# Which engine issues the loads of q, k, v and the stores, in a fused attention and expert kernel

## The chip, the cores and the metric

The kernel runs on one core of a Trainium2 chip. The core has a matrix engine (TensorE; PE in the profile, PEld its weight loads), VectorE (DVE), ScalarE (ACT), GpSimd (POOL) and SyncE (SP), each with its own instruction queue, which it works off in order, and 16 DMA engines, which move data between the device's memory (DRAM) and the on-chip memory (SBUF). An engine that issues a DMA does so at that place of its queue: if the DMA has to wait, say for a buffer to be free, all that stands behind it in the queue waits too. The metric is the time of one execution on the device in microseconds (us), lower is better.

## The reference

Three parts, all in float32, one after the other:

```
A  = softmax(q  @ mean18(k)^T / 8)          q, k, v: 4 batches x 8 heads x 576 tokens x 64
Bm = softmax(mean18(q) @ mean18(k)^T / 8)   mean18: means of 18 tokens, so 32 landmarks
C  = softmax(mean18(q) @ k^T / 8)
Z  = six Newton steps  Z <- 2Z - Z Bm Z     (pseudo-inverse of Bm)
x  = A Z C v                                2304 tokens x 512
e  = argmax of normalised x against 8 expert embeddings;  g = its softmax weight
x  = g * relu(x @ w1[e]) @ w2[e]            w1: 512 x 1024
x  = rmsnorm(x) * rms_g
out = (silu(x @ w_gate) * (x @ w_val)) @ w_out      512 -> 1536 -> 512
```

## The kernel before, in words

Batches b = 0 to 3 go through the first two parts one behind the other, and the stages of several batches overlap. A batch is handled in two halves of four heads (`hh`).

- `load` (L247) brings k and q of one half, 128 rows of 18 x 64 numbers (4,608 contiguous bytes a row, 576 KB), into one of two buffers each. `loadv` (L254) brings v of a batch, 1.1 MB, into the one v buffer: 128 rows with 8 runs of 1 KB each, and a tail of 64 rows with 8 runs of 256 bytes.
- `turn` (L262) transposes k and q on VectorE, `sums` (L277) makes the landmark sums (for batches 0 and 1 on TensorE, L285, later on VectorE or GpSimd, L310 to L315), `crow` (L334) computes C and its product with v (`pv`, L398), `inverse` (L406) the Newton steps (L465), `arow` (L542) the rows A. L598 in `arow` normalises these on GpSimd; TensorE then transposes them (L610).
- `pair` (L726) splits the turned rows into two float16 parts, `etp`, and stores them to DRAM as `ed`, and the small matrix WTb as `wd`. These copies are read again only by a slow path at the end (L1077, L1079), which runs when the tokens of some batch are not all for one expert.
- `logits` (L628) finds the expert of a batch. `Expert.load` (L911) reads its number on SP (L915) and then loads w1 and w2 of that expert, four tiles `raw` of 512 KB each (L922), into five buffers. `first` (L944) multiplies w1 by WTb (`pP`, L960), `rows` evicts that to `Pt` (ACT L968, then VectorE L970), `hidden` (L974) makes the hidden layer (`ph`, L994), `second` (L1010) the result (`pz`, L1033), and `out` (L1058) evicts a tile `y` on ACT (L1064) and stores it to DRAM as `yd` (L1068): 5 stores a batch, 20 in all.
- The last stage (`phase3`, L1373) reads yd back (`prep3`, L1281), normalises, transposes by DMA, converts its weights (r, L1201, to `W3.conv`), and makes the gated layer out of products of 128 x 128 blocks (L1542), with evictions by ACT (L1417, L1423, L1447) and VectorE (L1420, L1426, L1451), and the last product (L1517). `last` (L1460) evicts a tile `o` (ACT, four times VectorE) and stores it: 16 stores of 18, the last two are at L1624.

The order of all instructions is made when the program is built. The class `Order` (L28) runs every stage as a generator that yields an engine and an estimated time (`"P"`, `"V"`, `"A"`, `"G"`, and `"D"` for a DMA), `"wait"` for a token, `"get"` for a buffer, or `"lag"`, which shifts the time from which its next step may be placed. It always places the step that can begin first, and the instructions enter their engines' queues in the order of placement. All DMAs are placed on the one resource D, whichever engine issues them. Almost all of them are issued by SP; the two small loads of `embed` (L753, L754) and one of the last two stores are issued by ACT, and none by GpSimd.

Of the kernel before, what the change touches and what calls it, by code (L numbers as in the profile page):

```python
# [193 lines left out]
def phaseA(tc, ctx, c2, I, st, Jobs):  # L194

    nc = tc.nc
# [25 lines left out]
    def sb(shape, name, n=2, dt=F32, tag=None):  # L222
        if name in ("ae", "ce"):
            k = count[name] = count.get(name, -1) + 1
            at, w = dict(ae=(0, 1152), ce=(2304, 576))[name]
            at += w * (k % 2)
            v = x0[:, at:at + w]
            return v.rearrange("p (c l) -> p c l", l=32) if name == "ae" else v
        return (pe if name in ("q", "k", "v", "kT", "ts") else p1).tile(shape, dt, name=name, bufs=bufs.get(name, n), tag=tag or name)
# [16 lines left out]

    def load(b, hh, src):  # L247
        yield "get", src
        yield "D", 1.89
        t = T[src, b, hh] = sb([128, 18, 64], src)  # L250
        nc.sync.dma_start(t, I[src][b, 4 * hh:4 * hh + 4].rearrange("h (l j) d -> (h l) j d", j=18))
        R.sig(src, b, hh)

    def loadv(b):  # L254
        yield "get", "v"
        yield "D", 3.78
        t = T["v", b] = sb([128, 8, 5, 64], "v")
        nc.sync.dma_start(t[:, :, 0:4].rearrange("p h c d -> p h (c d)"), I["v"][b, :, 0:512, :].rearrange("h (s c) d -> s h (c d)", c=4))
        nc.sync.dma_start(t[0:64, :, 4], I["v"][b, :, 512:576, :].rearrange("h s d -> s h d"))
        R.sig("v", b)  # L260

    def turn(b, hh, src):  # L262
# [463 lines left out]
    def pair(b):  # L726

        yield "wait", ("et", b)
        yield "get", "etp"
        tp = T["etp", b] = p2.tile([128, 2, 2, 576], F16, name="etp", bufs=bufs["etp"])  # L730
        for hh in range(2):
            yield "beside", 0
            yield "A", 0.67
            A.copy(tp[:, hh, 0], T["et", b, hh])
            yield "GW", (1.3, 0.76)
            either(nc, R).tensor_tensor(out=tp[:, hh, 1], in0=T["et", b, hh], in1=tp[:, hh, 0], op=ALU.subtract)
            R.share("et", b, NET, 2)
            R.sig("etp", b, hh)
        yield "D", 1.80
        nc.sync.dma_start(st["ed"][b], tp)  # L740
        yield "wait", ("WTb", b)
        yield "D", 0.36
        nc.sync.dma_start(st["wd"][b], st["WTb"][:, b])

    def embed():

# [61 lines left out]
    for b in range(B):  # L808
        for hh in range(2):
            add(load(b, hh, "k"), "lk", b)  # L810
            add(load(b, hh, "q"), "lq", b)
            add(sums(b, hh, 1, "q"), "q", b)
            add(sums(b, hh, 0, "k"), "k", b)
            add(turn(b, hh, "k"), "tk", b)
            add(landmarks(b, hh), "lm", b)
            add(turn(b, hh, "q"), "tq", b)
            add(crow(b, hh), "crow", b)
        add(loadv(b), "loadv", b)
        add(inverse(b), "inv", b)
        add(arow(b), "arow", b)  # L820
        add(logits(b), "lgt", b)
        for c in range(5):
            add(xtile(b, c), "xt", b)
        add(pair(b), "pair", b)
        ex.add(b)
# [65 lines left out]
class Expert:  # L891
# [166 lines left out]
    def out(self, b, c, pz, r0, n):  # L1058
        nc, R, st = self.nc, self.R, self.st
        yield "wait", ("sel", b)  # L1060
        yield "get", "y"
        yield "A", 0.69
        y = self.tile("y", [128, 512], F32)
        nc.scalar.activation(y[r0:r0 + n], pz[r0:r0 + n], AF.Copy, scale=st["sel"][r0:r0 + n, 5 * b + c:5 * b + c + 1])  # L1064
        R.put("m")
        yield "D", 0.85
        t0 = 576 * b + 128 * c
        nc.sync.dma_start(st["yd"][t0:t0 + n, :], y[r0:r0 + n])  # L1068
        R.put("y")
        R.sig("yd", b, c)  # L1070

# [84 lines left out]
def either(nc, R):  # L1156
    return nc.gpsimd if R.eng == "G" else nc.vector
# [213 lines left out]


def phase3(tc, ctx, I, st, out, stg, w3, R=None):  # L1373
    nc = tc.nc
    A, V = nc.scalar, nc.vector
# [15 lines left out]
    def op(eng, cost, fn, waits=(), gets=(), puts=(), shares=(), sig=None):  # L1391
        for w in waits:
            yield "wait", w
        for g in gets:
            yield "get", g
        yield eng, cost
        fn()
        for g in puts:
            R.put(g)
        for g in shares:  # L1400
            R.share(*g)
        if sig:
            R.sig(*sig)
# [56 lines left out]
    def last(p, t, g, po):  # L1460
        o = None

        def copy():
            nonlocal o
            if g == 5:
                o = bp.tile([128, 512], F32, name="o") if p < len(PT) - 1 else st["o2"][:, 512 * t:512 * t + 512]
            else:
                o = part[t] = bp.tile([128, 512], F32, name=f"part{t}", bufs=1)
            if (p, g) == (0, 5):
                V.scalar_tensor_tensor(out=o, in0=po, scalar=1.0 / SW, in1=part[t], op0=ALU.mult, op1=ALU.add)  # L1470
            else:
                A.activation(o, po, AF.Copy, scale=1.0 / SW)  # L1472
            R.put(f"po{t}")

        yield from op("V" if (p, g) == (0, 5) else "A", 0.69, copy, gets=["o"] if g == 5 and p < len(PT) - 1 else [])
        if g < 5 or p == len(PT) - 1:
            return
        yield "D", 0.85
        n = PT[p][t]
        nc.sync.dma_start(out[128 * n:128 * n + 128, :], o)  # L1480
        R.put("o")

    def products():
# [4 lines left out]
        for p, gs in todo:  # L1488
# [9 lines left out]
            for s in SEQ:  # L1498
                if isinstance(s, int):
                    if om is None:  # L1500
                        continue
                    (p1, g1), b1 = om
                    t, g = (s, g1[0]) if len(g1) == 1 else (s // 2, g1[s % 2])
                    yield "beside", 0
                    first, final = g == 0 or (p1, g) == (0, 4), g == 5 or (p1, g) == (0, 3)
                    if first:
                        yield "get", f"po{t}"
                    yield "wait", ("l0", (p1, g1))
                    yield "wait", ("l1", (p1, g1))
                    yield "wait", ("w", "out", g)  # L1510
                    yield "P", 1.28
                    if first:
                        po[t] = ps3.tile([128, 512], F32, name=f"po{t}", bufs=1)
                    wo, u2 = w3.w["out", g], b1["u2"]
                    for i in range(2):
                        for j, (a, b) in enumerate(((0, 0), (0, 1), (1, 0))):
                            nc.tensor.matmul(po[t], lhsT=u2[:, a, i, 128 * s:128 * s + 128], rhs=wo[:, b, i], start=(first and i == 0 and j == 0), stop=(final and i == 1 and j == 2))  # L1517
                    R.share("u2", (p1, g1), 4)
                    if final:
                        R.add(last(p1, t, g, po[t]), 0)  # L1520
                    continue
# [45 lines left out]


def build(tc, I, out):
    nc = tc.nc  # L1570
    with ExitStack() as ctx:
# [16 lines left out]
        def begin(R):  # L1588

            c3 = a["c3"] = ctx.enter_context(ExitStack())  # L1590
            pool = c3.enter_context(tc.tile_pool(name="w3", bufs=1, reuse_waits="tile"))
            stg = c3.enter_context(tc.tile_pool(name="stg", bufs=2, reuse_waits="tile"))
            w3 = W3(tc, pool, stg, I, jobs)
            operands(nc, R, st, w3, stg)

            def enter():
                for b in range(B):
                    for c in range(5):
                        yield "wait", ("yd", b, c)
                yield "G", 0.01  # L1600
                a["c2"].close()
                a["nr"] = nc.values_load(st["nr"][0:1, 0:1], min_val=0, max_val=NT)
                phase3(tc, c3, I, st, out, stg, w3, R)

            R.add(enter(), 10000)
# [47 lines left out]
```

## Time and profile before

| | us |
|---|---|
| median of 3 runs (707.61 to 709.91) | 708.36 |
| the profiled execution | 706.84 |
| its span, first to last instruction | 705.1 |
| TensorE busy | 675.0 (96%) |
| VectorE busy | 447.7 (63%) |
| ACT busy | 366.7 (52%) |
| GpSimd busy | 86.4 (12%) |
| mean granted TensorE clock | 0.988 |

The span is that of one profiled execution; all moments are in us from its start. A row of the table by stage gives a stretch, its length, the busy time of PE, PEld, DVE, ACT and POOL with their instructions (x), the granted TensorE clock (1.00 is 2.4 GHz, 0.50 is 1.2 GHz), the mean busy share of the 16 DMA engines and what they moved in GB/s. A row of a timeline gives start, length, engine (with a q: its sequencer, as for a DMA's issue), line, operation, output<-inputs, shapes and the number of instructions merged, and in brackets the engine's idle time before it and what ended it. A row of waits names who waited, the line, for whom, and the total, the number and the longest. The length of a DMA row is that of its issue; the time to landing is given apart.

### The profile page before, as it was taken

To read this page: it belongs to the slowest core of one execution; us is meant where nothing else is said; L and a number is where in the kernel's file an instruction comes from. 1 tells how busy PE (TensorE), PEld (TensorE's weight loads), DVE (VectorE), ACT (ScalarE), POOL (GpSimd) and SP (SyncE) were. 2 spreads that over 40 slices of the span, in tenths; PEclk is the share of its full clock that TensorE was granted. 3 is DMA by queue.
4 is the path that set the end of the run, shared out by engine and by line. 5 is a ranking of instruction groups with operands and counts; after the bars stand their busy time and mean duration, and the time that the engine had idled before them with its cause. 6 is when DMAs were issued, how large, how long until landed. Compare 5 with 4: busy or idle time off the path is not lost. (4 is left out here: it accounts for less than half of the span.)

```text
span 705.1 us, 14424 instructions
## 1 busy us (share of the span) xinstructions
PE 675.0 (96%) x5779; PEld 470.0 (67%) x5779; DVE 447.7 (63%) x1067; ACT 366.7 (52%) x852; POOL 86.4 (12%) x107
## 2 busy tenths in 40 slices
PE   8989699999989999989999999999999999999994
PEld 7956378655635546467777777777777777777772
DVE  7798487644797998878888644365554543443331
ACT  2436387544867957556666544454444453333331
POOL 1033493010301401001110000000000000000000
PEclk9999799999999999999999999999999999999998
DMA  9264625524776884675232010543034040000100
GB/s 323 83 197 174 216 73 160 191 106 137 229 275 183 256 217 143 194 194 120 90 113 79 27 46 1 122 104 120 1 83 113 1 113 1 1 1 1 62 3 33
DMA packets 65436, 80.86 MB, mean 115 GB/s; under 512 B 38216, under 2 KB 42824, under 8 KB 65360
## 3 DMA queue, kind: packets, MB, share of 16 engines
q1 hardware_dynamic: 65184, 79.58, 37.6%
q8 instruction: 47, 0.77, 0.4%
q10 hardware_dynamic: 176, 0.28, 0.1%
q14 instruction: 29, 0.24, 0.1%
HBM read 59.26 MB, written 12.32 MB: 102 GB/s over the span
## 5 line engine op out<-in xcount | busy, mean ns | idle before, releaser
L1517 PE MATMUL po<-w_out,u 128*128 128x512 f16 x648 | 157.2, 379 | 0.3 <-ACT u L1447 0.2
L1542 PEld LDWEIGHTS <-w_gate 128*128 128x128 f16 x1260 | 114.5, 98 | 37.8 <-issue 3.5
L1542 PEld LDWEIGHTS <-w_val 128*128 128x128 f16 x1260 | 113.9, 98 | 12.4 <-issue 0.6
L1517 PEld LDWEIGHTS <-u 128*128 128x128 f16 x648 | 62.7, 98 | 54.8 <-ACT u L1447 0.7
L1420 DVE SCALAR_TENSOR_TENSOR cgate<-ps_gateb,cgate 128x256 f32<-128x256 f32 x81 | 34.3, 424 | 98.1 <-ACT cgate L1417 94.4
L1033 PE MATMUL pz<-w2p,hT 128*128 128x512 f16 x384 | 87.0, 380 | 2.2 <-DVE Pt L970 2.2
L1542 PE MATMUL ps_gatea<-x,w_gate 128*128 128x256 f16 (+1 forms) x720 | 88.9, 262 | 0.0
L1542 PE MATMUL ps_vala<-x,w_val 128*128 128x256 f16 (+1 forms) x720 | 88.6, 262 | 0.0
L1417 ACT ACTIVATE cgate<-ps_gatea 128x256 f32<-128x256 f32 x81 | 31.0, 383 | 105.7 <-PE ps_gatea L1542 105.1
L1033 PEld LDWEIGHTS <-hT 128*128 128x128 f16 x384 | 36.0, 98 | 51.6 <-issue 7.3
L1542 PE MATMUL ps_gateb<-x,w_gate 128*128 128x256 f16 (+1 forms) x540 | 67.0, 263 | 3.0 <-DVE cgate L1420 2.3
L1542 PE MATMUL ps_valb<-x,w_val 128*128 128x256 f16 (+1 forms) x540 | 67.1, 263 | 0.5 <-DVE cval L1420 0.5
L1447 ACT CAST u<-cval 128x512 f16<-128x512 f32 x54 | 33.4, 618 | 41.1 <-DVE cval L1426 22.9
L994 PE MATMUL ph<-etp,Pt 128*128 128x288 f16 x384 | 50.9, 289 | 0.3 <-DVE hT L1006 0.3
L1451 DVE TENSOR_TENSOR u<-cval,u 128x512 f16<-128x512 f32 x54 | 38.0, 703 | 13.7 <-ACT u L1447 11.5
L994 PEld LDWEIGHTS <-Pt 128*128 128x128 f16 x384 | 37.3, 99 | 12.6 <-issue 2.4
L1426 DVE TENSOR_TENSOR cval<-cval,cgate 128x256 f32<-128x256 f32 x81 | 35.2, 434 | 9.2 <-ACT cgate L1423 1.6
L1417 ACT ACTIVATE cval<-ps_vala 128x256 f32<-128x256 f32 x81 | 31.0, 383 | 17.9 <-PE ps_vala L1542 17.9
L1420 DVE SCALAR_TENSOR_TENSOR cval<-ps_valb,cval 128x256 f32<-128x256 f32 x81 | 34.1, 421 | 9.6 <-ACT cval L1417 8.9
L1423 ACT ACTIVATE cgate<-cgate 128x256 f32<-128x256 f32 x81 | 33.4, 413 | 3.3 <-DVE cgate L1420 3.3
L1006 DVE SCALAR_TENSOR_TENSOR hT<-ph,hT 128x288 f16<-128x288 f32 x64 | 27.7, 451 | 10.8 <-ACT hT L1004 9.7
L1004 ACT ACTIVATE hT<-ph 128x288 f16<-128x288 f32 x64 | 25.7, 408 | 11.8 <-PE ph L994 10.1
(236 smaller groups left out, 932.2 us busy)
## 6 DMA issues: line engine op xcount, KB each, us to landing
raw<-moe_w SPq DMA_DIRECT2D x32, 512.0 KB, 4.7
y<-yd SPq DMA_DIRECT2D x36, 256.0 KB, 3.1
r<-moe_w_gate SPq DMA_DIRECT2D x12, 512.0 KB, 4.0
r<-moe_w_val SPq DMA_DIRECT2D x12, 512.0 KB, 3.6
r<-moe_w_out SPq DMA_DIRECT2D x12, 512.0 KB, 4.6
k<-k SPq DMA_DIRECT2D x8, 576.0 KB, 4.0
q<-q SPq DMA_DIRECT2D x8, 576.0 KB, 5.7
v<-v SPq DMA_DIRECT2D x4, 1024.0 KB, 6.9
```

What stands on the lines that cost most here:

```text
L994: nc.tensor.matmul(ph, lhsT=P[:, g, a, 128 * j:128 * j + 128], rhs=x[:, g, c, 288 * n:288 * n + 288], start=(q == 0), stop=(q == 5))
L1004: nc.scalar.activation(h[:, 0, sl], ph, AF.Relu)
L1006: nc.vector.scalar_tensor_tensor(out=h[:, 1, sl], in0=ph, scalar=0.0, in1=h[:, 0, sl], op0=ALU.max, op1=ALU.subtract)
L1033: nc.tensor.matmul(pz, lhsT=h[:, a, s0:s0 + n], rhs=w[:, e, i], start=(j == 0 and q == 0), stop=(j == 6 and q == 5))
L1417: return lambda: (start(nm) if (i, h) == (1, 0) else None, A.activation(c[nm][:, i, h], banks[nm + ab][:, 0:m], AF.Copy, scale=C))
L1420: return lambda: V.scalar_tensor_tensor(out=c[nm][:, i, h], in0=banks[nm + "b"][:, 0:m], scalar=C, in1=c[nm][:, i, h], op0=ALU.mult, op1=A ...
L1423: return lambda: A.activation(c["gate"][:, i, h], c["gate"][:, i, h], AF.Silu)
L1426: return lambda: either(nc, R).tensor_tensor(out=c["val"][:, i, h], in0=c["val"][:, i, h], in1=c["gate"][:, i, h], op=ALU.mult)
L1447: A.copy(u[0][:, 0, i], c["val"][:, i].rearrange("p h m -> p (h m)"))
L1451: return lambda: either(nc, R).tensor_tensor(out=u[0][:, 1, i], in0=c["val"][:, i].rearrange("p h m -> p (h m)"), in1=u[0][:, 0, i], op=AL ...
L1517: nc.tensor.matmul(po[t], lhsT=u2[:, a, i, 128 * s:128 * s + 128], rhs=wo[:, b, i], start=(first and i == 0 and j == 0), stop=(final and i ...
L1542: nc.tensor.matmul(o, lhsT=wt[:, a, kk, w, 128 * (g % 2):128 * (g % 2) + 128], rhs=xT[:, b, 2 * x + kk, 0:m], start=(first and q == 0), st ...
```

## The change

Three groups of DMAs are issued by another engine, and v's load is cut differently:

- k, q and v of batches 1 to 3 are issued by GpSimd, those of batch 0 by SP as before. v comes in three DMAs, two of four heads and the tail.
- In the order, v's load may be placed only 4 us after its buffer is free (`"lag", 4`); the lag 0 of k and q shifts nothing. The times of the resource D stay as they were.
- `ed` is stored by GpSimd; `wd`, `yd` and `out` (the 16 of `last`) are stored by ACT.

```diff
     def load(b, hh, src):
         yield "get", src
+        yield "lag", 0
         yield "D", 1.89
         t = T[src, b, hh] = sb([128, 18, 64], src)
-        nc.sync.dma_start(t, I[src][b, 4 * hh:4 * hh + 4].rearrange("h (l j) d -> (h l) j d", j=18))
+        (nc.gpsimd if b > 0 else nc.sync).dma_start(t, I[src][b, 4 * hh:4 * hh + 4].rearrange("h (l j) d -> (h l) j d", j=18))
         R.sig(src, b, hh)
     def loadv(b):
         yield "get", "v"
+        yield "lag", 4
         yield "D", 3.78
         t = T["v", b] = sb([128, 8, 5, 64], "v")
-        nc.sync.dma_start(t[:, :, 0:4].rearrange("p h c d -> p h (c d)"), I["v"][b, :, 0:512, :].rearrange("h (s c) d -> s h (c d)", c=4))
-        nc.sync.dma_start(t[0:64, :, 4], I["v"][b, :, 512:576, :].rearrange("h s d -> s h d"))
+        for h in (0, 4):
+            (nc.gpsimd if b > 0 else nc.sync).dma_start(t[:, h:h + 4, 0:4].rearrange("p h c d -> p h (c d)"), I["v"][b, h:h + 4, 0:512, :].rearrange("h (s c) d -> s h (c d)", c=4))
+        (nc.gpsimd if b > 0 else nc.sync).dma_start(t[0:64, :, 4], I["v"][b, :, 512:576, :].rearrange("h s d -> s h d"))
         R.sig("v", b)
...
-        nc.sync.dma_start(st["ed"][b], tp)
+        nc.gpsimd.dma_start(st["ed"][b], tp)
         yield "wait", ("WTb", b)
         yield "D", 0.36
-        nc.sync.dma_start(st["wd"][b], st["WTb"][:, b])
+        nc.scalar.dma_start(st["wd"][b], st["WTb"][:, b])
...
-        nc.sync.dma_start(st["yd"][t0:t0 + n, :], y[r0:r0 + n])
+        nc.scalar.dma_start(st["yd"][t0:t0 + n, :], y[r0:r0 + n])
...
-        nc.sync.dma_start(out[128 * n:128 * n + 128, :], o)
+        nc.scalar.dma_start(out[128 * n:128 * n + 128, :], o)
```

## Rows read from the trace of the kernel before

**Rows 1.** The table by stage: stretch, length, busy times, clock, DMA share, GB/s.
```profile
60.00:70.70 10.70, 10.68 (x146) 6.87 (x145) 10.42 (x22) 6.66 (x19) 4.18 (x6) 1.00 0.62 215
70.70:77.70 7.00, 0.00 (x0) 0.00 (x0) 2.39 (x8) 0.00 (x0) 4.99 (x8) 0.69 1.02 315
77.70:84.30 6.60, 6.58 (x21) 2.46 (x22) 3.48 (x4) 1.78 (x3) 0.90 (x1) 0.55 0.64 236
100.00:180.00 80.00, 79.29 (x908) 51.47 (x905) 49.96 (x172) 46.07 (x120) 15.09 (x18) 1.00 0.45 143
180.00:302.00 122.00, 119.47 (x695) 62.65 (x695) 104.72 (x226) 87.63 (x173) 20.75 (x19) 1.00 0.70 210
...
313.00:696.30 383.30, 382.50 (x3113) 282.93 (x3110) 210.72 (x477) 182.43 (x429) 14.71 (x13) 1.00 0.22 58
```

**Rows 2.** TensorE's waits over the whole run, the first three of the list.
```profile
PE pP L960 <- DMA raw<-moe_w: 7.0, 1, 7.0
PE ps_gateb L1542 <- DVE cgate L1420: 2.3, 1, 2.3
PE pz L1033 <- DVE Pt L970: 2.2, 1, 2.2
```

**Rows 3.** Timeline of SP's queue, 59 to 71 us.
```profile
59.23 0.65 SPq L922 DMA_DIRECT2D raw<-moe_w  x1
61.88 0.34 SPq L251 DMA_DIRECT2D k<-k  x1
62.42 0.88 SPq L922 DMA_DIRECT2D raw<-moe_w  x2
68.88 0.39 SPq L258 DMA_DIRECT2D v<-v  x1
...
70.84 0.46 SPq L922 DMA_DIRECT2D raw<-moe_w  x1
```

**Rows 4.** Waits of SP's queue: the first from 60 to 75 us, the second overall.
```profile
SPq L258 <- PE pv L398: 5.5, 1, 5.5
...
SPq L740 <- POOL etp L736: 19.6, 1, 19.6
```

**Rows 5.** Timeline of TensorE, 68 to 90 us.
```profile
68.75 1.93 PE L960 MATMUL pP<-raw,WTb 128*64 128x512 f32 x6
77.72 1.97 PE L960 MATMUL pP<-raw,WTb 128*64 128x512 f32 x2 [7.03 <-DMA raw<-moe_w]
...
81.74 2.54 PE L994 MATMUL ph<-etp,Pt 128*128 128x288 f16 x12
84.12 1.04 PE L610 MATMUL pt<-idn,x 128*128 128x128 f32 x8
...
88.22 1.64 PE L994 MATMUL ph<-etp,Pt 128*128 128x288 f16 x12
```

**Rows 6.** Landing of raw, of k and q, of v; between, the v tail's issue (ns).
```profile
DMA to landing us min/median/max: 3.4/4.7/9.2
...
DMA to landing us min/median/max: 3.7/4.7/7.7
...
L259 SPq DMA_DIRECT2D v<-v x4: 617/970/1972, 3.3 to 115.3; - x4
...
DMA to landing us min/median/max: 6.1/6.9/9.9
```

**Rows 7.** Timeline of VectorE, 72 to 82 us.
```profile
72.36 0.74 DVE L970 SCALAR_TENSOR_TENSOR Pt<-pP,icS,Pt 128x512 f16<-128x512 f32 x1
80.44 0.75 DVE L970 SCALAR_TENSOR_TENSOR Pt<-pP,icS,Pt 128x512 f16<-128x512 f32 x1 [7.35 <-ACT Pt L968]
```

**Rows 8.** Timeline of GpSimd, 69 to 76 us.
```profile
69.75 1.29 POOL L310 TENSOR_TENSOR ts<-qT 128x576 f32<-128x576 f32 x1 [4.27 <-DVE lr L402]
...
72.90 2.13 POOL L598 TENSOR_TENSOR x<-x,sa 128x1152 f32<-128x1152 f32 x1
```

**Rows 9.** A DMA issued by ACT: duration in ns, minimum, median, maximum.
```profile
L753 ACTq DMA_DIRECT2D emb<-moe_expert_emb x1: 587/587/587, 0.7 to 0.7; - x1
```

**Rows 10.** L364 on VectorE, 55 to 130 us: duration in ns, minimum, median, maximum.
```profile
L364 DVE TENSOR_SCALAR rs<-sm x6: 151/159/1255, 57.7 to 129.0; 128x2 f32<-128x2 f32 x6
```

## The prediction

> **What bounds the kernel now.** I read the table by stage first, then TensorE's waits, then the queue of SyncE (SP) around the largest of them, then the engines that would be late next. The table [rows 1] splits the run at about 302 us. From 313 us to the end TensorE works 382.5 of 383.3 us at the full clock, and from 100 to 302 us it works 79.29 of 80 and 119.47 of 122 us. There only a smaller amount of work or a broken stretch could move the end, and the change touches no matmul. What is left lies in front: between 70.7 and 77.7 us TensorE does nothing at all, ACT nothing, VectorE (DVE) 2.39 us, and in the stretch behind it the granted clock is 0.55 of full, so the lower of the two levels (1.2 GHz) for most of it.
>
> The list of TensorE's waits names the cause [rows 2]: one wait of 7.0 us of the expert product pP (L960) on a load of raw, the first expert weight. The next two waits are 2.3 and 2.2 us, both on DVE. The SP queue shows why that load was late [rows 3]: SP issues the first raw tile at 59.23, a k load at 61.88, two more raw tiles from 62.42, and then a v load at 68.88, before the fourth raw tile at 70.84. In that stretch SP stood 5.5 us for that v load, for the one v buffer, which the product pv (L398) of the batch before had still to read [rows 4]. The raw tile behind it needed no such thing: the pool has five raw buffers, and only three tiles were out. So the wait is one of order in a queue, and the load then travelled beside 1.1 MB of v. TensorE had done its part by 70.68 and stood until 77.72 [rows 5].
>
> **The change part by part.**
>
> *The k, q and v loads of batches 1 to 3 go to GpSimd (POOL): 6 of k, 6 of q, 3 x 3 of v.* In SP's queue the load of the expert number is then followed by five raw loads with no wait between them (five buffers). The first three cost 0.65 and 0.88 us to issue [rows 3], so a fourth follows 2 us behind the first: about 61 us in place of 70.84. A raw load lands 3.4 to 9.2 us after its issue over all 32 of them [rows 6], so the fourth is there between 64.5 and 70.2 us. TensorE wants it at 70.7, after the six matmuls that start at 68.75 [rows 5]. Even the far end of the landings is in time, and I take the whole wait of 7.03 us as gone.
>
> What is late next? The first ph (L994) needs the third Pt, which goes pP, ACT, DVE. In the old run the third DVE part started at 80.44, as soon as ACT's was done [rows 7], and ph at 81.74. In the new run the second DVE part still stands at 72.36 to 73.10, so the third ends at 73.85 and ph can start at 73.9: 7.84 us earlier. From there the clock matters. Twelve ph took 2.54 us at the lower level from 81.74 and took 1.64 us at full speed from 88.22 [rows 5]. Without the long stop I expect no fall of the clock, since before this stop it stood at 1.00 and fell during it [rows 1]: another 0.9. **Sum of this edit: 8.7 us.**
>
> What carries it to the end: from 70.7 to 77.7 us DVE and ACT were idle too [rows 1], so neither has a backlog to work off, and everything behind moves up together.
>
> *What POOL pays.* POOL takes 25 DMAs more, the four ed stores among them. The trace has no DMA on POOL, so I bound it. From below: an issue on SP takes 0.34 to 0.65 us, and the v tail, 64 x 8 short rows, 0.62 to 1.97 [rows 3, 6]. From above: POOL is held until the bytes have landed, 3.7 to 7.7 us for k and q, 6.1 to 9.9 for v [rows 6]. Outside of some 58 to 76 us this is covered by POOL's idle time: it is busy 15.09 of 80 us from 100 to 180 [rows 1], and the loads have time, since buffers are two deep. Inside it one instruction counts: the normalisation L598, 72.90 to 75.03 [rows 8], whose result TensorE transposes (L610) at 84.12 [rows 5]. After the gain L610 wants to run at 75.4, so the cover is only 0.4 us. Queued behind the waiting v load on POOL are, at most, L598 and the q sums of batch 2 (which ACT takes up only after the third Pt). The three v issues, 0.39 + 0.39 + 0.97 us, would put L598's end at 76.8, 1.4 us late, if they stand ahead of it; the planner's new lag of 4 us moves v from its release at 68.9 to about 72.9, the time of L598, so they stand as likely behind, where they cost it nothing. Held to the landing of v (6.9 us, the median of its first part) L598 would end at 81.9, 6.5 us late. I take **0.5 us**, near the issue times, as those are the nearest rows, and keep 0 and 6.5 for the range.
>
> *ed to POOL, wd to ACT.* SP stood up to 19.6 us in front of an ed store [rows 4], with the last tile of w2 behind it; but TensorE had other work all the while, and no wait of it on that tile is in its list [rows 2]. I cost it at nothing.
>
> *yd and out stores on ACT (20 + 16, with wd 40).* Each makes ACT wait for its own result and then issue. The longer of the two DMAs that ACT issues at the start took 0.59 us [rows 9]. Forty at 0.59 are 24 us of ACT, spread over 550 us. Queued behind each are the next eviction of a PSUM bank or conversion; TensorE and DVE wait for these. ACT is busy 87.63 of 122 us in the expert stage and 182.43 of 383.3 us in the last one [rows 1], and TensorE has several banks in hand, so I take 0. Uncovered, all 24 us would appear; a tenth would be 2.4. SP loses these 40 waits, and that may gain: at most the 2.2 and 2.3 us of the other two waits of TensorE [rows 2].
>
> *The v load of batch 0 in three parts on SP:* one issue more, 0.4 us; no wait of TensorE on v is in its list [rows 2], and I cost it at 0.
>
> **Sum against the profiled execution:** 706.84 us (span 705.10 and 1.74 around it) - 8.7 + 0.5 = 698.6. The median of the runs is 708.36, 1.5 us above that execution: **700.2 us**.
>
> A rule of the Trainium skill speaks against this: the page "DMA: Bandwidth & Descriptors", section "Issuing engines are not separate DMA queues", says that DMAs of all engines end up on the same 16 DMA engines and that using several issuers saves only issue time. By that the fourth raw tile would come forward by the issue times of k and v alone (0.34 + 0.39 + 0.97, some 1.7 us) and the run end at 706.7; rows 4 show a wait of the issuer on a semaphore there, which the rule does not speak of.
>
> **The rivals.**
> *B, the transfer is the limit.* If raw waits for the DMA engines and not for SP, its fourth tile shares them with k, q and v, whoever issues them. For: the engines are full (1.02) from 70.7 to 77.7. Against: before that, from 60 to 70.7, they are 0.62 busy, which leaves 4 us of them, and one tile at 315 GB/s takes 1.7 [rows 1]. If it lands at 74, 3.3 us of the stop and the low clock remain, 3.7 are won: 704.7. 12%.
> *C, given back later.* TensorE comes to the last stage 8 us early, but DVE, busy 104.72 of 122 us there, has not converted the weights: the wait on DVE of 2.3 us [rows 2] grows to 10, and the whole gain is gone: 708.4. For: DVE is the fullest engine but one. Against: its work is also 8 us early. 12%.
> *D, more goes.* The two waits on DVE go as well, because SP's weight loads no longer stand behind stores: 4.5 us more and, with nothing lost on POOL, 0.5: 695.2. 13%.
> *A, POOL holds the front (slower).* POOL generates the DMAs slowly and its own arithmetic stands behind them. From a delay of L598 of 9.1 us on (84.12 less 75.03) L610 is later than before, whatever raw does. Held until landing, k, the v parts and q (3.7 + 6.9 + 7.7 = 18.3 us) put it 9.2 us late, 717.6, and three quarters of that 4.6 us late: 713.0. For: DVE and POOL can lock each other out; the tiny L364 takes 1.255 us at worst, 0.159 at the median [rows 10], and at its worst it ran beside L310 on POOL. Against: L598 in the old run starts right behind POOL's other work, and nothing says that POOL is held to the landing. 11%. The Trainium skill (page "SBUF — State Buffer", section "SBUF: two separate sides") says that GpSimd cannot write descriptors while DVE is in a two-port mode; no DMA of POOL is in this trace, so it shows only that the lock exists.
>
> **How the numbers follow.** My forecast, the first stop gone and a little lost on POOL, has 52%, its own range 697 to 703. About 0.3%, 2.1 us, is what runs of this kernel can tell from no change. Forecast, D and B end faster by more: 0.77. C is no change: 0.12. A is slower: 0.11. Range for 8 of 10: from just beyond D at 694 to 709, where C is inside, which leaves out A and the far side of D.
>
> **What would show it.** Right: in the new trace no TensorE idle time of 7 us near 70, the granted clock 1.00 from 60 to 100 us, five raw issues on SP within some 3 us of each other near 60, the stretch from 313 us on as long as now and started 8 us earlier. L598 ending by 77 shows that POOL's part is small; a TensorE wait on L598's result in front of L610 shows A. ACT's stores: TensorE's busy time in the last stage below 382 of the same length would show that they are not hidden. The prediction is wrong if the fourth raw tile still lands after 72 us, or if another wait of several us and a fall of the clock stands in the same place.

## The result and the profile after

The changed kernel takes 717.16 us (715.84 to 718.47, 4 runs) against 707.99 us for the kernel before on the same chip: 1.0119 times as long, 95% interval 1.0089 to 1.0148. The ratios here and below are formed over the fast executions alone (slow ones took, for example, 885 and 1003 us for the kernel before and 3,923 us with v back on SP) and can differ from the quotient of the two medians by some 0.003. The changed kernel is slower, where 700.2 us was forecast; 717.6 us was the price of rival A. The profiled execution spans 713.8 us, 8.7 us more than the 705.1 us of the kernel before. Its lines are 1 to 3 higher than in the kernel before (L598 is L601, L610 is L613, L994 is L997, the raw loads are L925, v is L261 and L262); where nm is rewritten below, one more.

First the part that the forecast was about. In SP's queue (start, length, instruction, count) the five raw loads follow each other, where k and v stood between them in [rows 3]:

```profile
65.07 2.73 SPq L925 DMA_DIRECT2D raw<-moe_w  x5
```

TensorE no longer waits for raw at all. The head of its list of waits (sum, times, longest):

```profile
PE pc L349 <- ACT kT L334: 9.1, 2, 7.7
PE pt L613 <- POOL x L601: 2.7, 2, 2.5
PE pP L963 <- DVE Pt L973: 2.6, 2, 1.5
...
PE pv L401 <- DMA v<-v: 2.1, 1, 2.1
```

Against [rows 2] the wait of 7.0 us is gone and three long ones are new: 7.7, 2.5 and 2.1 us. New too are the 2.6 us of pP for Pt; they stand where the raw stop was, ahead of ph, and are a part of what is left of it. TensorE's timeline shows the first two, with the idle time before each group in brackets; its ph at 79.58 is the one at 81.74 in [rows 5].

```profile
48.56 1.12 PE L613 MATMUL pt<-idn,x 128*128 128x128 f32 x4 [2.51 <-POOL x L601]
...
79.58 1.69 PE L997 MATMUL ph<-etp,Pt 128*128 128x288 f16 x12 [0.78 <-ACT Pt L971]
81.52 1.09 PE L613 MATMUL pt<-idn,x 128*128 128x128 f32 x8 [0.24 <-POOL x L601]
...
95.06 1.43 PE L349 MATMUL pc<-kT,kq 128*128 128x320 f32 x2 [7.75 <-ACT kT L334]
```

Who holds them is in GpSimd's timeline, first around 40 and then around 86 us. Each v load is three issues of 0.7 to 0.8 us, and ahead of the second and third GpSimd does nothing for some 4 us; the page's word for it, "issue", means that it waited for nothing that the profile shows.

```profile
35.34 0.83 POOL L261 DMA_DIRECT2D v<-v  x1 [0.61 <-PE pv L401]
40.44 0.76 POOL L261 DMA_DIRECT2D v<-v  x1 [4.27 <-issue]
45.08 0.72 POOL L262 DMA_DIRECT2D v<-v  x1 [3.89 <-issue]
45.79 0.56 POOL L252 DMA_DIRECT2D q<-q  x1
46.37 2.14 POOL L601 TENSOR_TENSOR x<-x,sa 128x1152 f32<-128x1152 f32 x1
...
81.40 0.81 POOL L261 DMA_DIRECT2D v<-v  x1
86.11 0.77 POOL L261 DMA_DIRECT2D v<-v  x1 [3.89 <-issue]
90.65 0.71 POOL L262 DMA_DIRECT2D v<-v  x1 [3.78 <-issue]
91.37 0.62 POOL L461 TENSOR_TENSOR bdm<-Bm,mask 128x256 f32<-128x256 f32 x1
91.94 0.37 POOL L318 TENSOR_TENSOR lm<-ts 128x64 f32<-128x64 f32 x1
```

Read it downwards: x (L601) can only start when the last part and a q load are out, and TensorE's L613 waits for x. In the second stretch a sum of 0.37 us (L318) stands behind all three parts; ACT waits for it, and TensorE for ACT. ACT's timeline ends the chain:

```profile
92.34 0.40 ACT L332 ACTIVATE kq<-lm,mask 128x128 f32<-128x128 f32 x1 [8.87 <-POOL lm L318]
...
94.76 0.24 ACT L334 COPY kT<-lm 128x64 f32<-128x64 f32 x1
```

The third v load does the same from 125.21 to 135.79 us, and there it is v itself that is late: its last part lands 3.6 us after its issue at 135.08, at about 138.7, and pv waits 2.1 us.

The table by stage (columns as in [rows 1]) shows the two stretches in front, the low clock behind the second, and the last stage:

```profile
46.00:54.40 8.40, 5.89 (x33) 5.37 (x32) 7.03 (x5) 2.81 (x8) 6.04 (x7) 0.60 0.62 195
87.30:95.10 7.80, 0.06 (x2) 0.04 (x1) 0.13 (x2) 2.76 (x9) 4.28 (x7) 0.80 0.28 84
95.10:98.80 3.70, 3.70 (x8) 2.46 (x8) 1.19 (x3) 3.18 (x6) 3.54 (x5) 0.50 0.00 0
...
321.60:705.00 383.40, 382.26 (x3109) 282.59 (x3107) 213.53 (x480) 183.88 (x430) 12.84 (x14) 1.00 0.23 61
```

The last stage is as long as in [rows 1], 383.4 against 383.3 us with the same 382 us of TensorE, so the stores that ACT now issues cost nothing there. Half of the clock's full speed (0.50, the lower level) stands where TensorE had just done nothing for 7.7 us.

The balance, from the start of the same TensorE instruction in both traces: +1.1 us by 21 us (start of the run); +5.95 behind the first hold; +5.7 at the eighth pP, then -2.2 at ph and -2.55 behind it, where the raw stop was (a gain of 8.2); +7.3 behind the second hold (a loss of 9.85); about +10 behind the third; +9.3 in the last stage.

### The profile page after: what moved, and what is told of

Its sections match the earlier page's. It is cut to its first block, busy times and chain, and to the rows that moved or that the text cites. A ratio compares the mean times of both kernels' runs of the same rounds, so it can differ in the third digit from the quotient of the medians.

```text
span 713.8 us, 14418 instructions
## 1 busy us (share of the span) xinstructions
PE 678.0 (95%) x5779; PEld 473.0 (66%) x5779; DVE 452.4 (63%) x1077; ACT 365.6 (51%) x849; POOL 86.0 (12%) x122
## 5 line engine op out<-in xcount | busy, mean ns | idle before, releaser
L997 PE MATMUL ph<-etp,Pt 128*128 128x288 f16 x384 | 50.0, 286 | 0.8 <-ACT Pt L971 0.8
L997 PEld LDWEIGHTS <-Pt 128*128 128x128 f16 x384 | 36.9, 98 | 12.0 <-issue 1.9
```

The source lines that it names most:

```text
L997: nc.tensor.matmul(ph, lhsT=P[:, g, a, 128 * j:128 * j + 128], rhs=x[:, g, c, 288 * n:288 * n + 288], start=(q == 0), stop=(q == 5))
```

## The experiments

Theory H: GpSimd is held behind each v part until room for its DMA descriptors is free, and this costs more than the raw stop gives. The rival at first: what GpSimd or ACT pay for is the number of issues, or the planner's new order, whatever the room. The first four runs shared a chip, on which the kernel before took 709.26 us.

**More room for the descriptors.** The changed kernel with one number changed:

```diff
-dynamic_dma_scratch_size=1024
+dynamic_dma_scratch_size=2048
```

> The changed kernel with one number changed: dynamic_dma_scratch_size 2048 in place of 1024, so twice the room for the descriptors of DMAs that GpSimd issues. Theory (ring): GpSimd is held between the three parts of each v load because the descriptors of two parts (each 512 runs) do not fit into the room together, so the next part waits until the one before has landed. Then the three parts follow each other here within about 1 us each (2.5 us in place of 10 from the first issue to the end of the last), TensorE's idle times of 2.5 us near 46, 7.7 us near 87 and 2.1 us near 137 go, and the time is near 701 us (717 less 3.5, 9.9 and 3). Rival (GpSimd waits for each landing, whatever the room): parts again 4 to 5 us apart, 717 us.

Measured: 708.74 us, ratio 0.9999 (0.9964 to 1.0034). GpSimd's timeline: the parts of v follow each other with no idle time between them.

```profile
34.29 1.57 POOL L261 DMA_DIRECT2D v<-v  x2 [0.40 <-PE pv L401]
35.86 0.72 POOL L262 DMA_DIRECT2D v<-v  x1
```

The issues are as long as before (0.71 to 0.82 us each over the nine); only the holds are gone, and with them the three long new waits. This shows the cause of the loss, and it rules out both rivals: the number of issues and the planner's order are the same here, and a part of v goes out before the one ahead of it has landed. What the room is for is read from that number's name; that its size decides is measured. But it only brings the kernel back to even, where 701 us were expected: in the stretch that was 89 to 98 us in the kernel before TensorE was 4.4 us early, and behind it 1.5 late. The head of its waits names the place:

```profile
PE pen L504 <- ACT WTb L496: 4.7, 2, 4.3
```

**v back on SP.** The changed kernel, v as two loads from SP, still four units later in the planner's order:

```diff
-        for h in (0, 4):
-            (nc.gpsimd if b > 0 else nc.sync).dma_start(t[:, h:h + 4, 0:4]...
-        (nc.gpsimd if b > 0 else nc.sync).dma_start(t[0:64, :, 4], ...
+        nc.sync.dma_start(t[:, :, 0:4]...
+        nc.sync.dma_start(t[0:64, :, 4], ...
```

> The changed kernel with v's loads of all batches back on SP in the two old DMAs; the lag of 4 us and all the rest stay. Theory (v's hold on GpSimd is the whole loss, and the lag puts v behind the raw tiles): no GpSimd hold, the five raw loads are issued together, no TensorE stop near 70 nor 87; near 700 us. Rival (SP's order is the point: v stands before raw there again): the stop of 7 us before pP comes back, 707 to 709 us.

Measured: 707.49 us, 0.9996 (0.9968 to 1.0024), where 700 were expected. No hold and no raw stop; TensorE 7.0 us early in the same stretch; and then the same new wait of 3.6 us on WTb. So that wait belongs neither to v on GpSimd nor to its room.

**The lag alone, and the stores alone.** Both from the kernel before:

```diff
+        yield "lag", 4          # in loadv
```

> The kernel before with only the lag of 4 us on v's load; all DMAs issued as before. Theory (order in SP's queue): if the lag carries v's load of batch 2 behind the raw tiles, the stop of 7 us goes and the time falls to about 700 us without any other issuer; if v stays between the raw tiles, 708 us and the same stop. Rival (the gain of the first stage needs other issuers): 708 us even with v behind the raw tiles.

Measured: 705.85 us, 0.9968 (0.9940 to 0.9996), between the two expectations. The raw stop shrinks from 7.0 to 4.0 us; SP now waits 6.4 us for q's buffer.

```diff
-        nc.sync.dma_start(st["ed"][b], tp)
+        nc.gpsimd.dma_start(st["ed"][b], tp)
...
+        nc.scalar.dma_start(...)          # wd, yd, out
```

> The kernel before with only the stores changed: ed by GpSimd; wd, yd and out by ACT; all loads by SP as before. Theory (the stores cost nothing and gain nothing): 707 to 709 us, and the same 7 us stop near 70. Rival (ACT's own issues delay evictions): the stretch behind 313 us longer by 2 us or more, 710 to 714 us.

Measured: 709.69 us, 1.0026 (0.9994 to 1.0059), a raw stop of 7.8 us. The stores are worth nothing measurable, in either direction.

**Who is late at WTb.** In the trace of the 2048-byte kernel ACT stands 5.04 us in front of the softmax x, waiting for nm, a VectorE product of 128 x 2 elements. VectorE's line and GpSimd's lines at the same time:

```profile
92.98 6.17 DVE L358 TENSOR_TENSOR nm<-mx,csc 128x2 f32<-128x2 f32 x1
```
```profile
92.18 6.28 POOL L943 TENSOR_TENSOR w2p<-raw,w2p 128x1024 f16<-128x1024 f32 x3
98.42 0.71 POOL L316 TENSOR_TENSOR ts<-ts 128x256 f32<-128x256 f32 x1
```

An instruction whose median is 0.161 us takes 6.17, from within GpSimd's first conversion to the end of the instruction behind the third (99.13). With v on SP it is 5.45 us, in the same place. By the code nm is the one VectorE operation there that reads two operands from SBUF; its neighbours read one from PSUM. The Trainium skill (page "SBUF — State Buffer", section "SBUF: two separate sides") says that a VectorE operation in a two-port mode, or one with two SBUF inputs against a GpSimd operation that reads SBUF, and the GpSimd operation exclude each other for a whole instruction. The trace agrees that nm is shut out, but it was shut out over four instructions of GpSimd, not one. Theory L from here on: it is this, and not the order of the queues. The test writes nm so that each product reads one operand from SBUF (a number takes the place of csc) and makes one column in place of two, in seven kernels:

```diff
-        V.tensor_tensor(out=nm, in0=mx, in1=csc, op=ALU.mult)
+        V.tensor_scalar(nm[:, 0:1], mx[:, 0:1], -0.125 / 18, None, ALU.mult)
+        V.tensor_scalar(nm[:, 1:2], mx[:, 1:2], -0.125 / 324, None, ALU.mult)
```

On the 2048-byte kernel:

> The changed kernel with the 2048-byte scratch for GpSimd's descriptors, and the product nm = mx * csc (VectorE, two SBUF operands) written as two products of one column each with a number (one SBUF operand each). Theory L (a VectorE operation with two SBUF inputs waits for as long as GpSimd's operations follow each other without a gap: nm took 6.17 us from 92.98 to 99.15 with the ring alone, while GpSimd ran 92.18 to 99.13, and 0.38 us in the kernel before, where there was a gap): nm 0.1 to 0.4 us in all, the stop of 4.33 us on TensorE ahead of pen is gone, TensorE's lead of 4.4 us at 89 to 98 us stays, and with the half clock that followed the stop some 5 us less: 703 to 705 us by the median. Rival Q (nm is only late by order: ScalarE's and GpSimd's queues are late there because of the DMAs they now issue): nm's place moves little, the stop stays over 3 us, 707 to 710 us.

Measured: 701.57 us (10 runs) beside 709.0 for the kernel before, 0.9886 (0.9854 to 0.9918), a little more than Theory L gave; rival Q is out. GpSimd's three conversions stand as they did, and nm passes beside the first of them. GpSimd's line, then VectorE's:

```profile
91.71 6.31 POOL L944 TENSOR_TENSOR w2p<-raw,w2p 128x1024 f16<-128x1024 f32 x3
```
```profile
92.58 0.14 DVE L358 TENSOR_SCALAR nm<-mx 128x1 f32<-128x1 f32 x1
92.64 0.14 DVE L359 TENSOR_SCALAR nm<-mx 128x1 f32<-128x1 f32 x1
```

The wait on WTb of 4.3 us is gone, and TensorE's lead ahead of that place (4.8 us) is still there 40 us later (4.5). On the kernel with v on SP:

> The changed kernel with v on SP in two parts (as before the change, but four units later in the order), and nm as two products with a number. Theory L: nm (5.45 us at 90.38 with v on SP alone) takes under 0.5 us, the stop of 3.60 us ahead of pen is gone, the lead of 7.0 us at 89 to 98 us stays to the end but for what the clock takes: 701 to 704 us. Rival Q: the stop stays, 706 to 708 us. Rival S (whatever lead the front gains is taken back at the next shared resource, the raw conversions on GpSimd): the stop is gone, but TensorE waits as long elsewhere before 130 us, 706 to 708 us.

Measured: 700.47 us, 0.9892 (0.9820 to 0.9964), with a lead of 4.5 us from 80 to 130 us; no wait takes its place, which rules out S. The control, the kernel before with nm alone:

> The kernel before, with nm alone as two products with a number. Theory L: nm was held for 0.38 us at most in the front, since GpSimd's operations left gaps, so there is nothing to gain: 707 to 710 us, the same within the interval; the stop of 7 us ahead of raw stays. Rival P (nm's form is worth something by itself, so that the two kernels above gain through it and not through the loads): 703 to 705 us.

Measured: 708.39 us, 0.9985 (0.9951 to 1.0019), the raw stop 6.7 us. The form of nm is worth nothing by itself. So nm was held by its form beside GpSimd's conversions, and not by the order of the queues; which property of the form, "Unsettled" below takes up. And on the changed kernel itself, room unchanged:

> The changed kernel with nm as two products with a number, the 1024-byte scratch kept. Theory H (the three holds of GpSimd behind v's second part set the end of the front by themselves; nm is not held there, since GpSimd starts its conversions of raw late, at 102.9 us): 715 to 718 us, as the changed kernel. Rival N (nm's hold is a part of the changed kernel's loss): 709 to 713 us.

Measured: 717.91 us, 1.0108 (1.0069 to 1.0147), beside 709.76 for the kernel before on that chip; two of the three waits are there (7.9 us on kT, 2.1 on v); the one on x is 0.8 us in place of 2.5, behind a clock that had already fallen at 43 us. In the changed kernel the holds alone make the loss; nm took 1.80 us at most there.

**Which parts of the change carry the gain.** k and q alone to GpSimd, from the kernel before:

```diff
-        nc.sync.dma_start(t, I[src][b, ...
+        (nc.gpsimd if b > 0 else nc.sync).dma_start(t, I[src][b, ...
```

> The kernel before with only k and q of batches 1 to 3 issued by GpSimd; v stays on SP at its old place in the order. Theory V (SP is held by its wait for v's buffer, 5.5 us from 59.9 on, so the lag on v is a part of the gain and k and q another): raw is issued late as before, a stop of 6 to 8 us ahead of raw stays on TensorE, 707 to 710 us. Rival K (taking k's and q's issues and waits off SP frees it enough): the stop is under 3 us, 703 to 706 us. Neither expects a hold on GpSimd: k's and q's 128 descriptors issued in 0.5 to 0.6 us each and one behind the other in the changed kernel.

Measured: 710.36 us, 1.0051 (1.0018 to 1.0084). SP's wait and TensorE's wait, from the two lists:

```profile
SPq L258 <- PE pv L398: 7.0, 1, 7.0
```
```profile
PE pP L960 <- DMA raw<-moe_w: 7.0, 1, 7.0
```

With k and q gone SP reaches v's wait sooner and stands there longer; nothing is won, and the kernel is, if anything, a little slower. The lag, with nm and all loads on SP:

> The kernel before with v four units later and nm as two products with a number, all loads on SP. With the lag alone the stop ahead of raw was 3.97 us in place of 7.03, SP waiting for q's buffer in place of v's, and the time 705.85 us. Theory V (k and q on SP keep a part of the stop): the stop is 3 to 5 us, 704.5 to 706.5 us; nm was not held there (0.38 us), so it adds nothing. Rival X (with nm free the lag alone gives all): 700 to 702.5 us.

Measured: 705.12 us, 0.9941 (0.9918 to 0.9964); now q holds SP and the stop is half as long:

```profile
SPq L251 <- DVE lr L404: 6.3, 1, 6.3
```
```profile
PE pP L962 <- DMA raw<-moe_w: 3.9, 1, 3.9
```

Lag, k and q on GpSimd, and nm together, all stores on SP:

> The kernel before with three edits: v four units later in the order (still on SP, two parts), k and q of batches 1 to 3 issued by GpSimd, nm as two products with a number. All stores stay on SP. Theory Z (the stores moved to ScalarE and GpSimd are worth nothing; lag, k and q, and nm are all of the gain): 699.5 to 702.5 us, as with the stores moved. Rival W (SP's wait for ed of batch 1 or its issues hold a raw load back): a stop ahead of a raw load past 90 us, 703 to 706 us.

Measured: 701.15 us (6 runs), 0.9897 (0.9864 to 0.9930). SP waits long for ed and v in this trace, as its list says, and TensorE never for what stands behind:

```profile
SPq L742 <- DVE etp L738: 27.2, 2, 21.7
...
SPq L259 <- PE pv L400: 9.0, 2, 6.5
```

So Z: the moved stores are no part of the gain. Of the edits run here this is the smallest that has all of it; k and q with nm but without the lag was not run. Last, the lag where v is GpSimd's, from the kernel with 2048 bytes and nm:

```diff
-        yield "lag", 4
```

> The changed kernel with the 2048-byte scratch and nm as two products, but v at its old place in the order (no lag of four units); v is still GpSimd's, in three parts. Theory G (the lag matters only while SP waits for v's buffer; on GpSimd the wait for the buffer comes earlier in its order and holds its sums and conversions instead): GpSimd stands before v's first part for some us, which shows as a stop on TensorE by a sum or x, 703 to 708 us. Rival I (the lag matters nowhere once v is off SP): 700.5 to 702.5 us, as with the lag.

Measured: 703.58 us (10 runs), 0.9898 (0.9864 to 0.9932), as with the lag (0.9886). GpSimd does stand 2.7 us for v's buffer at 72 us, but the longest new wait on TensorE is 1.05 us for x. So the cost is not where Theory G put it. The lag shows in another place. TensorE's wait of 2.3 us on cgate ([rows 2]) is 1.9 to 2.3 us in all five kernels without the lag and at most 0.5 us in one piece in the nine with it, also with the stores on SP; in its place those nine have one of 1.0 us on ACT's cgate. Here, and then in the kernel with the lag:

```profile
PE ps_gateb L1545 <- DVE cgate L1423: 2.1, 1, 2.1
```
```profile
PE ps_gateb L1546 <- DVE cgate L1424: 0.6, 2, 0.4
```

What that is worth stays open below some 2 us: by the medians (703.58, in Theory G's range, and 701.57) it is 2 us, by the two ratios nothing.

## Why the prediction was wrong

**Right: the raw stop.** Five raw issues within 2.73 us, no wait on raw, ph 7.84 us earlier against the run's own shift just before it. That this is the figure of the working to the hundredth is luck. The working let ph start when VectorE's third Pt is done; in the run that is at 80.19 us, and ph starts at 79.58, released by ACT's Pt (L971):

```profile
78.79 1.40 DVE L973 SCALAR_TENSOR_TENSOR Pt<-pP,icS,Pt 128x512 f16<-128x512 f32 x2
```

The clock gave 0.4 more where 0.9 was expected; 0.24 of the difference is the wait for x at 81.52. The step is worth 8.2 us, forecast 8.7. Rival B is out: the transfers were not the limit. So is the reading of issue time alone, some 1.7 us, that was worked out beside the Trainium skill's rule on issuing engines; the wait in SP's queue was what counted. With v on SP it took the lag as well as k and q: either alone gave at most half of it. With v on GpSimd and room for it the raw stop is gone without the lag too.

**Right: the stores.** Forecast at nothing; alone 1.0026 (0.9994 to 1.0059), and the last stage as long as before.

**Wrong: "What POOL pays", 0.5 us.** This step failed, in three ways. First its scope: it said that outside of some 58 to 76 us GpSimd's idle time covers the loads, from a busy share of 15.09 of 80 us. A share is no cover: one sum of 0.37 us behind the v parts held ACT, and by it TensorE. Only L598 of batch 1 was priced, and there the price was about right: TensorE waited 0.24 us for it (81.52). The holds struck x of batch 0 (46 us), a sum for batch 2 (92 us) and v of batch 3 (137 us). Second its size: the upper bound, held until landing, was the true mechanism in part, since the next v part goes out 0.3 to 0.4 us after the part before has landed (the one issued at 35.34 landed 4.7 us later, at 40.07, and the next went out at 40.44; 85.73 and 86.11 for the second load); for k and q it is not, those follow each other in 0.53 to 0.70 us. The bound was written down at 6.5 us for one place and then dropped from the chances in favour of the nearest rows, which were rows of SP: another engine, whose issues say little of GpSimd's. Third its count: three loads, each a hold of some 10 us. Rival A described this, at 11%, but for another instruction. That its price (717.6) lies beside the measured 717.16 us is luck: it is one hold of 18.3 us ahead of L598 without any gain, and the run has three holds (4.9, 9.85 and some 2.7 us of TensorE's time) and the gain of the raw stop against them.

**Wrong as well: "everything behind moves up together".** Had the holds not been, the gain would still have been lost (708.74 us with more room). The argument was that neither DVE nor ACT had a backlog. The thing that was late next was neither a backlog nor a queue but two kinds of instructions that now fell on each other: nm and the conversions on GpSimd. The hint stood in [rows 10], 1.255 us for an instruction whose median is 0.159, beside GpSimd; the prediction used it only for what GpSimd pays. With the lock out of the way too, three kernels give 700.5, 701.2 and 701.6 us, ratios of 0.9886 to 0.9897. The forecast was 700.2 of 708.36 us, 0.9885: what the raw stop is worth when nothing new takes its place. That they meet it so closely is luck in part. Between 131 us and the last stage TensorE gains another 1.1 to 2.0 us in these three traces, where the waits on cgate and Pt of [rows 2] are gone or shorter. That is a part of what rival D expected, but not by its reason: with the stores alone moved these waits stay (1.9 and 2.2 us), and they go with the lag.

**Unsettled.** In the kernel before nm also met three conversions in a row without a gap (95.62 to 101.94 on GpSimd), and still came through behind the first:

```profile
97.39 0.38 DVE L355 TENSOR_TENSOR nm<-mx,csc 128x2 f32<-128x2 f32 x1
```

Why it was let in there and shut out over all of them in two other kernels, the runs don't tell. Theory L as it was written ("a gap") is too simple. Nor is the second SBUF operand shown to be what makes nm wait: the new form has one operand, but also one column in place of two and another operation. In the kernel before L364, the instruction of [rows 10], reads one tensor operand (`V.tensor_scalar(rs, sm, 1e-9, None, ALU.add)`) of two columns, and it was held to the end of GpSimd's L310 all the same. VectorE's line, then GpSimd's:

```profile
62.00 1.25 DVE L364 TENSOR_SCALAR rs<-sm 128x2 f32<-128x2 f32 x1 [0.15 <-ACT Be L361]
```
```profile
61.93 1.30 POOL L310 TENSOR_TENSOR ts<-kT 128x576 f32<-128x576 f32 x1 [6.97 <-DVE kT L269]
```

That the new form frees nm is shown; that one operand would be enough is not, and no run has two columns with one operand in nm's place. Nor is the first hold's price clean: the low clock between 41 and 55 us came in some kernels without any stop over 0.9 us there (+2.8 us with more room), so of the 4.9 us only the stop of 2.5 is surely the hold's.

## What to carry to other kernels

Before a load moves to GpSimd, list each instruction queued behind it there and who waits for it, and price the load by its hold, not by an issue on another engine; large loads in parts may need more room for descriptors (here 2048 bytes of scratch were enough and 1024 were not). When a stall goes, look at which instructions come to lie beside each other on VectorE and GpSimd: a tiny product that GpSimd shuts out can cost about as much as the stall did (here the rewritten nm gave 7 us, 708.74 to 701.57). If an in-order queue is blocked by one wait, first move that wait later in its own queue: the lag, with k and q elsewhere and one VectorE product rewritten, gives 1% (0.9897, 0.9864 to 0.9930) without any of the stores.

## What the runs showed of the hardware

- A first or second part of v (4 heads of 512 x 64 numbers, 0.52 MB) took GpSimd 0.76 to 0.83 us to issue; the next part started 4.5 to 5.4 us after it with 1024 bytes of scratch and 0.8 us after it with 2048. k and q were not held in that way: with 1024 bytes four of these loads went out between 13.54 and 16.13 us, and the first of them landed at 17.67.
- A VectorE product of 128 x 2 elements with two SBUF operands (nm) took 0.147 to 6.171 us in one run; with one operand, 128 x 1, 0.13 to 0.16 us in two kernels with GpSimd's conversions beside it. A VectorE sum of 128 x 2 elements with one tensor operand (L364) took 0.151 to 1.255 us, the longest beside GpSimd's L310.
- The stop of TensorE of 7.75 us cost more than its length: the lower clock (0.50) stood behind it until 98.8 us, and together they cost 9.85 us. The clock also fell to half, for some us between 41 and 55 us, in runs with no stop over 0.9 us there (0.50 from 45.8 to 52.6 us with more room).
- The first 36 products pj, the same in every kernel, took 4.3 to 6.9 us from profile to profile. By an estimate from this (2.4 us by 21 us) and the low clock around 45 us (2.8 us), the spans of two single profiles can differ by some 5 us without any effect of the change.
